# Row tiles of the second matmul in pairs and two rounds, convolution jobs ahead of the copies out

One kernel on one core of a Trainium2 chip. The metric is the device time in microseconds (us), the median over executions of the same program; the kernel before takes 698.73 us (6 executions, 698.49 to 698.90).

## The reference

A light convolution over time (7 taps, softmax weights per head), then a feed-forward block with a leaky ReLU:

```python
w = softmax(weight)                                 # [8 heads, 7 taps]
out[b, s, h, :] = sum_k w[h, k] * x[b, s + k - 6, h, :]   # x is [8, 4096, 192]
h = out.reshape(32768, 192) @ w_in                  # w_in  [192, 2048]
g = maximum(0.01 * h, h)
result = g @ w_out                                  # w_out [2048, 192]
```

## The kernel before

DVE (VectorE) does the convolution, PE (TensorE) both matmuls, ACT (ScalarE) the Prelu between them. The work is cut into 37 groups: ten half groups (256 time steps of two batches, `T = 256`), then 27 full ones (`T = 512`). In each step of the loop PE does two blocks of the first matmul (`mm1`), and then a quota of "slots" of the second matmul for the group before. Both matmuls use row tiling: the 128 rows of the array work as two tiles of 64 rows, which run beside each other.

A sum `po[n]` of the second matmul (128 tokens by 192 outputs) needs 16 chunks of 128 rows, each split into the upper and the lower 64. Both kernels keep the two row tiles out of each other's PSUM bank (the prediction names the page that asks for it). In the kernel before row tile 0 goes first through sum n, and row tile 1 follows 24 slots later; by then row tile 0 is in the bank of sum n+1 or n+2. A manual dependency, the "seal", makes row tile 1's first matmul wait for a Prelu that comes after row tile 0's last.

```python
    LAG = NFC + NFC // 2                 # NFC = 16: 24 slots
    ...
    LAST = NSUB - 2 * SUB - 1            # 247 of 256 sums go by row tiles
    ...
    def mm1(grp, u):
        ...                              # 12 matmuls, then the Prelu `act`
        while unsealed:
            seal[unsealed.pop()] = act.ins.name

    def mm2_slot(q):
        n, fc = divmod(q, NFC)
        if n < LAST:
            mm2_one(0, n, fc)            # row tile 0
        t1 = q - LAG
        if t1 >= 0:
            mm2_one(1, *divmod(t1, NFC)) # row tile 1; at fc == 0 it waits for seal[n]
            if t1 % NFC == NFC - 1:
                evac_o(t1 // NFC)        # copy out of PSUM: ACT in half groups, then DVE
    ...
        per = -(-len(ahead) // (steps - 1)) if T == ST else -(-len(ahead) // steps)
        for j in range(steps):
            ...                          # two blocks of mm1
            for _ in range(quota):
                mm2_slot(slot)
                slot += 1
            for job in ahead[per * j : per * (j + 1)]:
                job()                    # convolution of the next group, on DVE
    ...
    while slot < LAST * NFC + LAG:       # row tile 1 alone
        mm2_slot(slot)
        slot += 1
    for n in range(LAST, NSUB):          # the last sums with all 128 rows
        ...
```

## Time and profile before

| | before |
|---|---|
| time, median | 698.73 us |
| span of the profiled execution | 697.6 us |
| PE, DVE, ACT busy | 99%, 78%, 73% |

A line of the timeline or of the costliest groups has the source line, engine, operation and tiles; `x32` is a count. In the timeline the first number is the start and the second the time to the last end, both in us. PE's ends overlap the next starts, so I take a part's length from its start to the start of what follows. What to see before is shown in the prediction.

### The profile page before, as it was taken

What the parts mean: (1) busy time and instruction counts of PE and PEld (TensorE: products, weight loads), DVE (VectorE), ACT (ScalarE), POOL (GpSimd) and SP (SyncE); (2) the same over time, 40 slices, a digit from 0 to 9 for tenths busy, and PEclk for the clock granted to TensorE, in tenths of its full rate; (3) what the DMA queues carried; (4) which work ended last, traced back from release to release, by engine and by line L of the source; (5) the groups of instructions that cost most, each with busy time, mean ns of one, the idle gap of its engine ahead of it and who ended that gap; (6) DMA issues with size and microseconds to landing.
All of it is one profiled execution on the core that took longest, in us unless ns stands there. A gap on an engine that the chain in (4) does not pass through costs nothing.

```text
span 697.6 us, 26016 instructions
## 1 busy us (share of the span) xinstructions
PE 689.2 (99%) x11762; PEld 608.4 (87%) x11762; DVE 543.1 (78%) x1005; ACT 512.2 (73%) x576; POOL 139.6 (20%) x195
## 2 busy tenths in 40 slices
PE   8999999999999999999999999999999999999997
PEld 6799998678888888888888888888888888888887
DVE  6899999967777787777787777787777787777712
ACT  6788887977777777777777777777777777777770
POOL 3632221410222210222211222210222211000000
PEclk9999999999999999999999999999999999999999
DMA  9988553845566545556635556634566626122112
GB/s 171 108 97 96 83 77 77 85 72 81 73 71 92 81 69 81 70 72 90 84 65 82 68 77 85 87 69 75 76 75 82 91 63 77 55 52 58 47 36 70
DMA packets 184015, 54.39 MB, mean 78 GB/s; under 512 B 148320, under 2 KB 183136, under 8 KB 183904
## 3 DMA queue, kind: packets, MB, share of 16 engines
q0 software_dynamic: 97936, 14.17, 29.1%
q1 hardware_dynamic: 85968, 38.56, 22.6%
q8 instruction: 92, 1.51, 0.9%
q14 instruction: 19, 0.16, 0.1%
HBM read 29.88 MB, written 25.17 MB: 79 GB/s over the span
## 4 chain that ended last, share of the span: by engine, by line
PE 86%; DVE 11%; DMA 2%; ACT 1%; issue 1%; SPq 0%; ACTq 0%
PE po L388 43%; PE ph L367 41%; DVE yt L181 9%; DMA x_nat<-in_x_dram 1%; ACT g L374 1%; DVE yt L175 1%; PE acc L200 1%; PE warm L249 1%; DMA xt<-x_bf 1%; PE ptr L142 0%; DVE x_bf L127 0%; ACT x_bf L127 0%; DVE diag L296 0%; ACT yt L329 0%; SPq L430 0%
## 5 line engine op out<-in xcount | busy, mean ns | idle before, releaser
L374 ACT ACTIVATE g<-ph 128x1024 bf16<-128x1024 f32 x512 | 496.3, 1021 | 163.0 <-PE ph L367 163.0
L181 DVE SCALAR_TENSOR_TENSOR yt<-xt,wk,yt 128x512 bf16<-128x512 bf16 (+1 forms) x648 | 442.5, 683 | 17.6
L388 PE MATMUL po<-w_out,g 64*128 64x192 bf16 (+1 forms) x8048 | 397.9, 243 | 0.0
L388 PEld LDWEIGHTS <-g 64*128 64x128 bf16 (+1 forms) x8048 | 371.9, 94 | 29.0 <-issue 0.2
L367 PE MATMUL ph<-yt,w_in 64*128 64x512 bf16 (+1 forms) x3552 | 391.7, 347 | 2.1 <-ACT g L374 0.9
L367 PEld LDWEIGHTS <-w_in 64*128 64x128 bf16 x3552 | 247.4, 94 | 48.9 <-issue 5.6
L78 POOL DMA_DIRECT2D x_bf<-in_x_dram x180 | 133.6, 773 | 420.7 <-DMA xt<-x_bf 418.2
L427 DVE COPY o_sb<-po 128x192 f32<-128x192 f32 x216 | 77.3, 358 | 127.2 <-PE po L388 124.9
L175 DVE TENSOR_SCALAR yt<-xt,wk 128x512 bf16<-128x512 bf16 (+1 forms) x108 | 36.4, 337 | 0.3 <-DMA xt<-x_bf 0.3
L427 ACT COPY o_sb<-po 128x192 f32<-128x192 f32 x40 | 13.0, 325 | 0.0
L249 PE MATMUL warm<-zero 128*128 128x256 bf16 x24 | 5.8, 404 | 1.1 <-DVE junk L217 1.1
L200 PE MATMUL acc<-xt,diag 64*64 64x256 bf16 x84 | 6.6, 318 | 0.0
L200 PEld LDWEIGHTS <-diag 64*64 64x64 bf16 x84 | 5.2, 126 | 1.3 <-DVE xt L156 0.4
L249 PEld LDWEIGHTS <-zero 128*128 128x128 bf16 x24 | 2.8, 134 | 2.5 <-DVE junk L217 1.1
L304 ACT ACTIVATE diag<-ident,whm 128x64 bf16<-128x64 bf16 x14 | 3.6, 336 | 1.9 <-DVE whm L290 1.9
L156 DVE COPY xt<-ptr 128x384 bf16<-128x384 bf16 x7 | 2.2, 353 | 1.9 <-PE ptr L142 1.8
L474 POOL COPY pjunk<-g 1x1 bf16<-1x1 bf16 x1 | 0.2, 177 | 16.5 <-ACT g L374 16.5
L142 PEld LDWEIGHTS <-x_bf 64*128 64x128 bf16 x48 | 1.1, 101 | 2.7 <-ACT x_bf L127 1.9
L142 PE MATMUL ptr<-ident,x_bf 64*128 64x64 bf16 x48 | 1.6, 202 | 1.5 <-ACT x_bf L127 0.9
L127 DVE CAST x_bf<-x_nat 128x384 bf16<-128x384 f32 x5 | 2.3, 453 | 0.7 <-DMA x_nat<-in_x_dram 0.7
L329 ACT ACTIVATE yt<-acc,rsum 128x256 bf16<-128x256 f32 x2 | 0.9, 474 | 2.5 <-PE acc L200 2.5
L237 POOL DMA_DIRECT2D w_in<-in_moe_w_in_dram x4 | 2.6, 659 | 0.0
(34 smaller groups left out, 13.1 us busy)
## 6 DMA issues: line engine op xcount, KB each, us to landing
out_dram<-o_sb SPq DMA_DIRECT2D x128, 192.0 KB, 2.1
x_bf<-in_x_dram POOLq DMA_DIRECT2D x180, 64.0 KB, 3.1
x_nat<-in_x_dram SPq DMA_DIRECT2D x8, 192.0 KB, 4.3
w_in<-in_moe_w_in_dram POOLq DMA_DIRECT2D x4, 384.0 KB, 9.5
xt<-x_bf SPq DMA_TRANSPOSE x90, 2.4
w_out<-in_moe_w_out_dram POOLq DMA_DIRECT2D x1, 768.0 KB, 16.2
w<-in_weight_dram SPq DMA_DIRECT2D x1, 0.2 KB
```

Of the source, the lines that this page charges most:

```text
L78: nc.gpsimd.dma_start(out=t[:, c, :, e, :], in_=src[2 * rp + e, :, :, c * CH : (c + 1) * CH],)
L142: nc.tensor.transpose(out=ts[i][:, s, c, :], in_=x_bf[q // 2][ps, c, (q % 2) * HS + s, :, :].rearrange("p e k -> p (e k)"), identity=ident ...
L175: lambda s=src, d=dst, c=c: nc.vector.tensor_scalar_mul(d, s, wk[:, c, 0:1])
L181: lambda s=src, d=dst, c=c, k=k: nc.vector.scalar_tensor_tensor(out=d, in0=s, scalar=wk[:, c, k : k + 1], in1=d, op0=mybir.AluOpType.mult, ...
L200: lambda k=k, p=p, a=a, e=e, ps=ps: nc.tensor.matmul(out=acc[ps, :T], lhsT=diag[c][ps, p, k, :], rhs=xt[0][ps, c, a : a + T], start=(k == ...
L237: nc.gpsimd.dma_start(out=w_in[e * CH : (e + 1) * CH, :, fs], in_=moe_w_in[:, fs].rearrange("(c p) f -> p c f", p=CH),)
L249: nc.tensor.matmul(out=wa[:, 0, 0:HT], lhsT=zero[:, 0:128], rhs=zero, start=True, stop=True)
L304: nc.scalar.activation(out=diag[c][:, 1, k, :], in_=ident2, func=mybir.ActivationFunctionType.Copy, scale=whm[:, c, 1, k : k + 1],)
L367: nc.tensor.matmul(out=ph[:, e, i * T : (i + 1) * T], lhsT=w_in[ps, c, f * 128 : (f + 1) * 128], rhs=y[ps, c, t0 : t0 + T], start=(c == 0) ...
L374: act = nc.scalar.activation(out=g[blk][:, nf * u : nf * (u + 1), :, t0 : t0 + T], in_=ph.rearrange("p e (i t) -> p i e t", i=nf), func=my ...
L388: ins = nc.tensor.matmul(out=po[m], lhsT=g[b][ps, fc, e, s * 128 : (s + 1) * 128], rhs=w_out[ps, fc, :], start=(rt != 1 and fc == 0), stop ...
L427: copy(out=o_sb[:, n % 2, :], in_=po.pop(n))
```

## The change

Sums go in pairs through two rounds of 16 slots. In round 0 row tile 0 works on the first sum of the pair and row tile 1 on the second; in round 1 they change places. Both leave their banks at the same time, so there is no offset. Between the rounds stands one wait, for the copy out of the pair before. In full groups the convolution jobs stand ahead of the copies in DVE's order, spread over all eight steps.

```diff
-    LAG = NFC + NFC // 2
-    LAST = NSUB - 2 * SUB - 1
+    LAST = NSUB - 2 * SUB
...
+        p, fc = divmod(q, 2 * NFC)
+        rnd, fc = divmod(fc, NFC)
+        pair = (2 * p, 2 * p + 1)
+        first, last = fc == 0, fc == NFC - 1
...
+        for rt in range(2):
+            ins = mm2_one(
+                rt, pair[rt ^ rnd], fc, first and rnd == 0, last and rnd == 1
+            )
+            if first and rnd == 1:
+                sync(ins, seal, "both row tiles have left these banks")
+        if last and rnd == 0:
+            seal_round(p, ins)           # seal = evac_o(2 * p - 1), which waits for ins
+        if last and rnd == 1:
+            evac_o(pair[0])
...
+            if T == ST:
+                jobs = ahead[len(ahead) * j // steps : len(ahead) * (j + 1) // steps]
+                for job in jobs:
+                    job()
             for _ in range(quota):
                 mm2_slot(slot)
                 slot += 1
...
-    while slot < LAST * NFC + LAG:
-        mm2_slot(slot)
-        slot += 1
+    evac_o(LAST - 1)
```

More of the change, by code (lines that the diff above doesn't have):

```diff
@@ L345 @@
     evac_first(1, nc.vector.tensor_copy, nc.vector.tensor_copy)
-    g, po, osb, seal = {}, {}, {}, {}
+    g, po, osb, seal = {}, {}, {}, None
     subs = [
@@ L353 @@
     NSUB = len(subs)
-    LAST = NSUB - 2 * SUB - 1
-    unsealed = []
+    LAST = NSUB - 2 * SUB
     def mm1(grp, u):
@@ L378, in mm1, with sync, mm2_one @@
         )
-        while unsealed:
-            seal[unsealed.pop()] = act.ins.name
-        return act
-    def mm2_one(rt, m, fc):
+        return act
+    def sync(after, first, why):
+        tc.add_manual_dep(
+            after.ins, first.ins.name,
+            mybir.DependencyInfo(
+                mybir.DependencyClass.Sync, mybir.DependencyReason.DATA
+            ),
+            reason=why,
+        )
+    def mm2_one(rt, m, fc, start, stop):
         b, e, s = subs[m]
-        if rt != 1 and fc == 0:
-            po[m] = psum_o.tile([128, D], FP32, name="po", tag="po")
         ps = slice(0, 128) if rt is None else slice(rt * CH, (rt + 1) * CH)
-        ins = nc.tensor.matmul(
+        return nc.tensor.matmul(
             out=po[m],
@@ L391, in mm2_one, with mm2_slot, seal_round @@
             rhs=w_out[ps, fc, :],
-            start=(rt != 1 and fc == 0),
-            stop=(rt != 0 and fc == NFC - 1),
-        )
-        if rt == 0 and fc == NFC - 1:
-            unsealed.append(m)
-        if rt == 1 and fc == 0:
-            tc.add_manual_dep(
-                ins.ins, seal[m],
-                mybir.DependencyInfo(
-                    mybir.DependencyClass.Sync, mybir.DependencyReason.DATA
-                ),
-                reason="other row tile, same bank",
-            )
-    def mm2_slot(q):
-        n, fc = divmod(q, NFC)
-        if n < LAST:
-            mm2_one(0, n, fc)
-        t1 = q - LAG
-        if t1 >= 0:
-            mm2_one(1, *divmod(t1, NFC))
-            if t1 % NFC == NFC - 1:
-                evac_o(t1 // NFC)
+            start=start,
+            stop=stop,
+        )
+    def mm2_slot(q):
+        p, fc = divmod(q, 2 * NFC)
+        rnd, fc = divmod(fc, NFC)
+        pair = (2 * p, 2 * p + 1)
+        first, last = fc == 0, fc == NFC - 1
+        if first and rnd == 0:
+            for n in pair:
+                po[n] = psum_o.tile([128, D], FP32, name="po", tag="po")
+        for rt in range(2):
+            ins = mm2_one(
+                rt, pair[rt ^ rnd], fc, first and rnd == 0, last and rnd == 1
+            )
+            if first and rnd == 1:
[4 more added lines that the diff above has]
+            evac_o(pair[0])
+    def seal_round(p, ins):
+        nonlocal seal
+        if p == 0:
+            seal = nc.scalar.copy(out=junk, in_=junk)
+        else:
+            seal = evac_o(2 * p - 1)
+        sync(seal, ins, "between the rounds")
     def evac_o(n):
@@ L426, in evac_o @@
         copy = nc.scalar.copy if b < NHALF else nc.vector.tensor_copy
-        copy(out=o_sb[:, n % 2, :], in_=po.pop(n))
+        ins = copy(out=o_sb[:, n % 2, :], in_=po.pop(n))
         if n % 2 == 1:
@@ L433, in evac_o @@
             )
+        return ins
     pjunk = const_pool.tile([1, 1], BF16)
@@ L447 @@
             ahead = conv_jobs(groups[i + 1]) if i + 1 < len(groups) else []
-        per = -(-len(ahead) // (steps - 1)) if T == ST else -(-len(ahead) // steps)
+        per = -(-len(ahead) // steps)
         for j in range(steps):
@@ L462 @@
                     cast_first(3, u - 2, nc.scalar.copy)
+            jobs = ahead[per * j : per * (j + 1)]
+            if T == ST:
+                jobs = ahead[len(ahead) * j // steps : len(ahead) * (j + 1) // steps]
+                for job in jobs:
+                    job()
+                jobs = []
             for _ in range(quota):
@@ L477 @@
                 transpose_x(2)
-            for job in ahead[per * j : per * (j + 1)]:
+            for job in jobs:
                 job()
@@ L489 @@
         avail += 2 * T // 128 * NFC
-    while slot < LAST * NFC + LAG:
-        mm2_slot(slot)
-        slot += 1
+    evac_o(LAST - 1)
     for n in range(LAST, NSUB):
+        po[n] = psum_o.tile([128, D], FP32, name="po", tag="po")
         for fc in range(NFC):
-            mm2_one(None, n, fc)
+            mm2_one(None, n, fc, fc == 0, fc == NFC - 1)
         evac_o(n)
```

## The prediction

> **What bounds the kernel now.** I read the page first: busy shares, costliest groups, then the waits, then the timeline of single steps, and at the end the tail.
>
> ```profile
> PE 689.2 (99%) x11762; PEld 608.4 (87%) x11762; DVE 543.1 (78%) x1005; ACT 512.2 (73%) x576; POOL 139.6 (20%) x195
> L181 DVE SCALAR_TENSOR_TENSOR yt<-xt,wk,yt 128x512 bf16<-128x512 bf16 (+1 forms) x648 | 442.5, 683 | 17.6
> L388 PE MATMUL po<-w_out,g 64*128 64x192 bf16 (+1 forms) x8048 | 397.9, 243 | 0.0
> L367 PE MATMUL ph<-yt,w_in 64*128 64x512 bf16 (+1 forms) x3552 | 391.7, 347 | 2.1 <-ACT g L374 0.9
> L427 DVE COPY o_sb<-po 128x192 f32<-128x192 f32 x216 | 77.3, 358 | 127.2 <-PE po L388 124.9
> ```
>
> PE is busy 99% of the span and its two matmul lines wait 2.1 us in all; DVE's copies out wait for PE, not the other way. So PE sets the time, and the question is only whether it runs slots faster, or fewer of them. The timeline of PE in a stretch of full groups shows a step: 12 matmuls of 512 columns, then 16 slots of two 192-column matmuls, one per row tile.
>
> ```profile
> 402.02 1.56 PE L388 MATMUL po<-w_out,g 64*128 64x192 bf16 x32
> 403.34 1.53 PE L367 MATMUL ph<-yt,w_in 64*128 64x512 bf16 x12
> 404.64 1.56 PE L388 MATMUL po<-w_out,g 64*128 64x192 bf16 x32
> ```
>
> From start to start: the second matmul's 16 slots take 403.34 - 402.02 = 1.32 us, that is 82.5 ns a slot; the first's 12 take 1.30. A step is 2.62 us, with no gap between its parts. There are 256 steps, some 670 us of the 698.75. The chain that ended last shows the same, with one odd round:
>
> ```profile
> 660.33 1.29 PE ph L367 x12
> 661.63 1.36 PE po L388 x32
> 662.99 1.29 PE ph L367 x12
> 664.28 1.32 PE po L388 x32
> ```
>
> The first round of a full group takes 1.36 us instead of 1.32. The reason stands in the timeline of another such round: the Prelu ahead of it starts after 0.74 us of idleness, not 0.66 to 0.68, and it is the Prelu that "seals" a half-sum: row tile 1 may enter the bank in the middle of the round only when it is done.
>
> ```profile
> 409.56 1.94 ACT L374 ACTIVATE g<-ph 128x1024 bf16<-128x1024 f32 x2 [0.74 <-PE ph L367]
> 409.87 1.60 PE L388 MATMUL po<-w_out,g 64*128 64x192 bf16 x32
> ...
> 412.15 1.94 ACT L374 ACTIVATE g<-ph 128x1024 bf16<-128x1024 f32 x2 [0.66 <-PE ph L367]
> 412.52 1.56 PE L388 MATMUL po<-w_out,g 64*128 64x192 bf16 x32
> ```
>
> Such rounds come once a group, 20.96 us apart, from 200.27 to 661.39 us: (661.39 - 200.27) / 20.96 + 1 = 23 rounds.
>
> Last the tail. The row tiles run 24 slots apart, so row tile 1 has 24 slots left alone once row tile 0 is through; then 9 sums follow with all 128 rows, 144 matmuls:
>
> ```profile
> 679.81 14.13 PE L388 MATMUL po<-w_out,g 64*128 64x192 bf16 x168
> 681.88 11.83 PEld L388 LDWEIGHTS <-g 128*128 128x128 bf16 x144 [0.16 <-issue]
> 693.98 0.36 DVE L427 COPY o_sb<-po 128x192 f32<-128x192 f32 x1 [0.96 <-PE po L388]
> ```
>
> The lone slots start at 679.81 and the full ones at 681.88: 2.07 us for 24 slots of half work, 86 ns each, about the price of a whole pair.
>
> **What the Trainium skill says.** "TensorE: Matmul & The Clock Gate", section "Back-to-back issue gap", gives N / 2.4 + 2.5 ns: 82.5 ns for 192 columns, which is the slot of this trace to the digit, and 215.8 for 512 (1.295 us for six pairs; trace 1.30). Nothing is left to gain in a full slot. "TensorEngine Tiling (Array Packing)", section "Restrictions and Gotchas", says that different row tiles may not access one PSUM bank at the same time and software must see to it: hence the seal before, and the two rounds with a wait between them after. The trace agrees only in that the two tiles' slots do run beside each other with two banks open. The same page, "Key Properties", says a change of tiling mode drains the array; the trace has one change to 128 rows at the end, with 0.16 us of idle weight load. The change keeps exactly one. "Perfetto Trace Analysis", section "Identifying the Most-Contended Engine", warns that matmul busy time is a poor roofline measure; so I rest on start-to-start times, not on 99%.
>
> **The change, part by part.**
>
> 1. *No offset between the row tiles.* Pairs start and end together, so no lone slots. At the start this saves nothing: the loop gives a fixed 16 slots to each step of the second group, filled or half filled, and that stretch ends in a wait of 0.87 us for a cast on ACT. At the end: before, 24 lone slots plus 9 full sums of 16 = 168 slots after the last paired round; after, 16 paired slots (round 1 of the last pair, in the last step) plus 8 full sums = 144. Saved 24 x 82.5 ns = 1.98 us, and some 0.08 us more of the slower lone start. **-2.0 us**.
> 2. *The seal moves from the Prelu to the copy out.* The 0.04 us of 23 rounds goes, because a round's first slot no longer depends on the Prelu: **-0.9 us**. The new wait: round 1 needs a copy that itself waits for round 0's last matmul. But quotas are 16 slots a step (8 in one group), so rounds end with the step, and two first-matmul blocks, 1.30 us, lie before the next round. A copy now starts about 0.28 us after the start of the last matmul it waits for (its 243 ns and some 40), and takes 0.36: the seal is ready about 0.64 us after the round. Slack about 0.6 us. In the half groups ACT copies (0.33 us) and its next Prelu comes late enough: the same slack. **0**.
> 3. *Conv jobs ahead of the copies.* 21 jobs over 8 steps instead of 7, at most three multiply-adds a step. On DVE three of them follow each other in about 0.78 us and the copy occupies 0.27: 3 x 0.78 + 0.27 = 2.60 us of a step of 2.62. So DVE arrives at its copy just on time in the worst step, and does not fall behind. The last three jobs of a group end about 0.25 us after the last round; the first matmul of the new group that needs their chunk starts 0.43 us after it, and DVE to PE takes about 0.05 us where the trace shows such a wait. Slack about 0.12 us. **0**.
> 4. *Small things.* 16 matmuls more (one sum moves from full to half rows), already in part 1; one copy of 1 column on ACT in the second group, which idles 0.69 us there. Copies, transfers and bytes are unchanged. PE's instructions that wait fall from 1034 to 735 in the built program; satisfied waits show no cost in 1.32 us rounds that hold one. **0**.
>
> Sum: 698.75 - 2.0 - 0.9 = **695.8 us**, 0.4% faster, well within 2%.
>
> **The rivals.**
>
> *The seal becomes a wait.* If DVE comes to the copies over 0.6 us late, round 1 stalls. For it: three-job steps leave only 0.01 us. Against: they are never more than two in a row, then a short step follows, and before already fits three jobs and a copy in a step (idle before copies still sums to 124.9 us). A stall of 0.1 us in each of some 100 pairs of the full groups would be +10 us, about 706.
>
> *Groups start on late jobs.* Slack is only 0.12 us, and before the jobs had a whole step in hand. If the last job came 0.2 us after it is needed at 26 group starts, +5 us: about 701. Against: DVE's durations are the same to a few ns from group to group, and DMA-fed waits of these jobs sum to 0.3 us. An input arriving late would hit here first, since jobs start about 1.4 us earlier than now.
>
> *The tail gains nothing or more.* If the end hung on transfers out, the 2 us would vanish: 697.8. Against: 0.96 us idle before each copy of the tail, waiting for PE. If the lone slots at the start also cost, up to 2 us more: 694.
>
> **Range and chances.** The base is 695.8. Both new waits can only add, and their slack is known to about 0.1 us, so the range reaches further up: 695.0 to 697.6. Faster by over 2% would need 14 us and no view offers that: 0.01. Slower by over 2% needs a stall of over 0.1 us at every round: 0.02. Within 2%: 0.97.
>
> **What would show it.** Right: the chain has no 1.36 us rounds at group starts; the tail's matmuls are 128 full ones directly after a first-matmul block and one paired round; line L388's successor has 8064 matmuls; idle time of PE stays near 2 us. Wrong: first-matmul blocks longer than 1.30 us at group starts with DVE's conv line as releaser (part 3), or rounds longer than 1.32 us or starting late, with a DVE copy as releaser (part 2).

## More of the kernel before

To compare traces I cut PE's work at six starts that the timeline shows in every one: the first slot; the first `mm1` block of 512 columns; nine steps later, the second step of the second full group; the last `mm1` block; the last matmul; the end.

## The result

The kernel after takes 696.08 us (median of 6, 695.24 to 696.88), 2.65 us less. The ratio is 0.9961 with a 95% interval of 0.9948 to 0.9974. Ratios here are the mean time of one kernel's runs over that of the other's of the same rounds, so not quite the ratio of the medians. It is a gain clear of noise, well inside 2%, and 0.3 us from the predicted 695.8.

The busy line and three of the costliest groups after; the columns are busy us, mean ns of one, then idle time before them and what ended it.

```profile
PE 683.7 (99%) x11778; PEld 539.4 (78%) x11778; DVE 543.9 (78%) x1005; ACT 516.4 (74%) x577; POOL 139.7 (20%) x195
L391 PE MATMUL po<-w_out,g 64*128 64x192 bf16 (+1 forms) x8064 | 382.7, 243 | 0.0
L365 PE MATMUL ph<-yt,w_in 64*128 64x512 bf16 (+1 forms) x3552 | 379.3, 347 | 2.7 <-DMA w_in<-in_moe_w_in_dram 1.1
L438 DVE COPY o_sb<-po 128x192 f32<-128x192 f32 x216 | 77.1, 357 | 121.5 <-PE po L391 115.5
```

PE still fills 99%, with 16 matmuls more, and nothing on DVE or ACT has become the bound. The second matmul's line has no idle time: the new wait between rounds never shows. The chain that ended last, in the same part of the kernel as the one shown of before:

```profile
655.71 1.29 PE ph L365 x12
657.00 1.32 PE po L391 x32
658.32 1.29 PE ph L365 x12
659.62 1.32 PE po L391 x32
660.94 1.29 PE ph L365 x12
662.23 1.32 PE po L391 x32
```

No 1.36 us round is left. The timeline at a group start tells why: the Prelu is as late as before (0.74 us of idleness), but the round takes 1.32 us, from 408.40 to 409.72. It is the first round of its pair, and none of its matmuls and weight loads carries a wait in the trace. (In the trace of before, row tile 1's matmul of the ninth slot of such a round starts at 410.64, 0.06 us after the end of the Prelu that it waits for.) The wait stands at the head of the second round, whose first weight load starts at 410.80 and first matmul at 411.01; the copy that it waits for starts at 409.94 and is done at 410.29.

```profile
408.03 1.94 ACT L372 ACTIVATE g<-ph 128x1024 bf16<-128x1024 f32 x2 [0.74 <-PE ph L365]
...
408.40 1.50 PE L391 MATMUL po<-w_out,g 64*128 64x192 bf16 x32
...
409.94 0.36 DVE L438 COPY o_sb<-po 128x192 f32<-128x192 f32 x1 [1.21 <-PE po L391]
...
411.01 1.50 PE L391 MATMUL po<-w_out,g 64*128 64x192 bf16 x32
```

And the tail, in the timeline of PE and of the weight loads:

```profile
677.75 12.16 PE L391 MATMUL po<-w_out,g 64*128 64x192 bf16 x160
679.17 10.51 PEld L391 LDWEIGHTS <-g 128*128 128x128 bf16 x128 [0.16 <-issue]
```

One paired round (32 matmuls) and 128 full ones, where before 24 lone matmuls preceded 144. The six stretches of the two profiled executions:

| stretch, us | before | after | difference |
|---|---|---|---|
| start to first slot | 23.92 | 23.37 | -0.55 |
| to the first 512-column block | 94.59 | 94.60 | +0.01 |
| nine steps | 20.30 | 19.79 | -0.51 |
| full groups, to the last `mm1` block | 539.63 | 538.69 | -0.94 |
| to the last matmul | 15.25 | 13.21 | -2.04 |
| to the end | 3.87 | 3.88 | +0.01 |
| span | 697.56 | 693.54 | -4.02 |

The profiles differ by 4.0 us where the medians differ by 2.65, because the profiled execution before took 699.26 us (above its median) and the one after 695.24 (the fastest of six). The extra lies in the first and third rows. The question for the experiments is which of these rows the change made.

### The profile page after: what moved, and what is told of

Read it like the earlier page. It is cut to its first block, busy times and chain, and to the rows that moved or that the text cites. A ratio compares the mean times of both kernels' runs of the same rounds, so it can differ in the third digit from the quotient of the medians.

```text
span 693.5 us, 26049 instructions
## 1 busy us (share of the span) xinstructions
PE 683.7 (99%) x11778; PEld 539.4 (78%) x11778; DVE 543.9 (78%) x1005; ACT 516.4 (74%) x577; POOL 139.7 (20%) x195
## 4 chain that ended last, share of the span: by engine, by line
PE 93%; DMA 3%; DVE 2%; ACT 1%; POOL 0%; issue 0%; SPq 0%; POOLq 0%; DVEq 0%
PE po L391 48%; PE ph L365 45%; DVE yt L180 2%; DMA w_in<-in_moe_w_in_dram 1%; DMA x_nat<-in_x_dram 1%; DMA xt<-x_bf 1%; ACT g L372 0%; POOL sel L226 0%; DVE yt L174 0%; ACT x_bf L126 0%; POOL w_in L236 0%; PE ptr L141 0%; DVE x_bf L126 0%; SPq L441 0%; POOL sel L224 0%
## 5 line engine op out<-in xcount | busy, mean ns | idle before, releaser
L391 PEld LDWEIGHTS <-g 64*128 64x128 bf16 (+1 forms) x8064 | 352.2, 94 | 45.3 <-issue 0.2
L391 PE MATMUL po<-w_out,g 64*128 64x192 bf16 (+1 forms) x8064 | 382.7, 243 | 0.0
L365 PE MATMUL ph<-yt,w_in 64*128 64x512 bf16 (+1 forms) x3552 | 379.3, 347 | 2.7 <-DMA w_in<-in_moe_w_in_dram 1.1
L365 PEld LDWEIGHTS <-w_in 64*128 64x128 bf16 x3552 | 186.5, 94 | 98.1 <-issue 4.6
L199 PE MATMUL acc<-xt,diag 64*64 64x256 bf16 x84 | 5.2, 270 | 0.5 <-DVE xt L155 0.5
```

The costliest lines, as they stand in the source:

```text
L199: lambda k=k, p=p, a=a, e=e, ps=ps: nc.tensor.matmul(out=acc[ps, :T], lhsT=diag[c][ps, p, k, :], rhs=xt[0][ps, c, a : a + T], start=(k == ...
L365: nc.tensor.matmul(out=ph[:, e, i * T : (i + 1) * T], lhsT=w_in[ps, c, f * 128 : (f + 1) * 128], rhs=y[ps, c, t0 : t0 + T], start=(c == 0) ...
L391: return nc.tensor.matmul(out=po[m], lhsT=g[b][ps, fc, e, s * 128 : (s + 1) * 128], rhs=w_out[ps, fc, :], start=start, stop=stop,)
```

## The experiments

My theory: the change is worth two terms, 0.94 us for the seal and 2.04 us for the tail; the start-up and the nine steps vary by themselves; the new wait and the new order cost nothing, because they have slack. The rivals: the 1.36 us rounds had another cause; lone slots cost something else than a full slot; the wait between rounds costs nothing in any position; the order of the jobs is a part of the gain.

### The seal alone: 25 slots apart instead of 24

The kernel before, with one edit:

```diff
-    LAG = NFC + NFC // 2
+    LAG = NFC + NFC // 2 + 1
```

> The kernel before with the row tiles 25 slots apart instead of 24. Theory (two separate savings: the seal's 0.04 us in 23 rounds, and 82.5 ns for each lone slot): the slot that waits for the Prelu comes 82.5 ns later, which is more than the 40 ns that it is late, so the 1.36 us rounds become 1.32 (23 x 0.04 = 0.92 us less), and one lone slot is added at the end (0.08 us more): 698.73 - 0.84 = 697.9 us. Rival (the 1.36 us rounds have another cause at group starts, such as the weights of the first round or the reuse of the g buffer by PE itself): they stay at 1.36 and the time is 698.8.

Measured: 698.48 us (697.47 to 699.11), ratio to before 0.9993, interval 0.9981 to 1.0006. The times alone say nothing, as they scatter by 1.6 us. The trace does: the full groups take 538.69 us, 0.94 less than before and to the digit what the kernel after takes. None of its 208 full rounds from the first 512-column block on is longer than 1.32 us. From its chain, where the round at 661.45 is the first of a group:

```profile
658.83 1.32 PE po L388 x32
660.15 1.29 PE ph L367 x12
661.45 1.32 PE po L388 x32
662.76 1.30 PE ph L367 x12
664.06 1.32 PE po L388 x32
```

So the 0.04 us were the wait for the Prelu; one slot more of distance removes it as well as the new scheme does. The interval of the ratio (1.3 us less to 0.4 us more) holds both the 0.84 us expected and no change. In the profiled execution the gain is hidden by the first slot, which came at 25.02 us, 1.1 later than in the profile of before: from 14.89 us on the granted clock was 0.50 for 3.4 us, and there 24 matmuls of `mm1` took 2.74 us, where before took 1.75.

### The price of a lone slot: 40 slots apart

```diff
-    LAG = NFC + NFC // 2
+    LAG = 2 * NFC + NFC // 2
```

> The kernel before with the row tiles 40 slots apart instead of 24. Theory: the seal lies a whole step before the slot that needs it, so no 1.36 us round is left (0.92 us less), and the tail has 40 lone slots, 16 more at 82.5 ns (1.32 us more): 698.73 - 0.92 + 1.32 = 699.1 us, and against the run with 25 slots 15 x 82.5 ns = 1.24 us more. The tail's matmuls from the last first-matmul block on: 40 lone slots in about 3.4 us, of which 16 in the last step. Rival (lone slots cost half, as they do half the work): 15 x 41 ns = 0.6 us more than with 25, 698.5 us. Rival (the offset at the start costs as well): 2.5 us more than with 25, about 700.4.

Measured: 700.18 us (699.02 to 700.57), ratio 1.0015, interval 1.0002 to 1.0027. Weight loads of the tail with 25 slots apart, then with 40:

```profile
679.38 2.21 PEld L388 LDWEIGHTS <-g 64*128 64x128 bf16 x25
681.74 2.34 PEld L388 LDWEIGHTS <-g 128*128 128x128 bf16 x29 [0.16 <-issue]
```

```profile
678.16 3.44 PEld L388 LDWEIGHTS <-g 64*128 64x128 bf16 x40
681.76 2.26 PEld L388 LDWEIGHTS <-g 128*128 128x128 bf16 x28 [0.16 <-issue]
```

From the first lone load to the first full one: 2.36 and 3.60 us. The 15 more lone slots cost 1.24 us, 82.7 ns each: the price of a full slot for half the work, as expected. The full groups take 538.69 us here too. The stretch between the first slot and the first 512-column block takes 94.36 us, so lone slots at the start cost nothing. The medians of these two runs differ by 1.70 us instead of 1.24, within their scatter; the profiled executions (699.11 and 699.28 us) differ by only 0.17, because the late first slot of the one with 25 (25.02 us against 23.73) takes up the 1.24.

### The wait between rounds without cover

The kernel after, with all rounds moved by 8 slots, so that a round ends in the middle of a step and the next one follows at once:

```diff
-        quota = (avail - slot) // steps
+        quota = (avail - slot - (8 if i > 1 else 0)) // steps
...
-            for _ in range(quota):
+            for _ in range(quota - (8 if i == 1 and j == 0 else 0)):
...
+    while slot < LAST * NFC:
+        mm2_slot(slot)
+        slot += 1
     evac_o(LAST - 1)
```

> The kernel after with its rounds moved by 8 slots, so that they end in the middle of a step and the next round follows at once, with no first matmuls between. Theory (the wait between the rounds is free only because 1.30 us of first matmuls cover it): every round 1 stalls for the copy: 0.28 us to its start, 0.36 us, 0.05 us to PE, so about 0.69 us in some 104 pairs of the full groups (72 us), and about 1.1 us in some 20 pairs of the half groups, where the copy stands behind two Prelus on ACT (22 us): about 790 us, rounds of 16 slots split into two parts with a gap of 0.7 us. Rival (PE's hardware or the early weight load hides the wait, or the copy is quicker seen from PE): under 720 us.

Measured: 780.91 us (780.41 to 780.99), ratio to before 1.1173. PE's timeline in a step, then two lines of the waits (us in total, times, longest):

```profile
433.87 0.82 PE L391 MATMUL po<-w_out,g 64*128 64x192 bf16 x16
435.15 0.83 PE L391 MATMUL po<-w_out,g 64*128 64x192 bf16 x16 [0.46 <-DVE o_sb L438]
435.82 1.46 PE L365 MATMUL ph<-yt,w_in 64*128 64x512 bf16 x12
```

```profile
PEld L391 <- DVE o_sb L438: 70.4, 103, 0.7
PEld L391 <- ACT o_sb L438: 20.8, 18, 1.2
```

Eight slots would take 0.66 us; the second eight start 1.28 us after the first eight. The stall is 0.62 to 0.64 us a pair in the full groups (the stretch grows by 604.27 - 538.69 = 65.6 us) and in the half groups it comes 18 times, and longer, from ACT (there the stretch grows by 113.50 - 94.60 = 18.9 us). Together 84.5 of the 84.8 us between the medians. The wait is real, and only its place makes it free. The sum was 9 us too high, 6 of them in the full groups: with both row tiles in step a copy starts 0.21 to 0.22 us after the round, not 0.28, so the wait is 0.22 + 0.36 + 0.05 = 0.63 us.

### Slack at the group starts

The kernel after, with one more multiply on DVE ahead of the last step's jobs:

```diff
                 jobs = ahead[len(ahead) * j // steps : len(ahead) * (j + 1) // steps]
+                if j == steps - 1 and jobs:
+                    nc.vector.tensor_scalar_mul(extra, extra, wk[:, 0, 0:1])
                 for job in jobs:
```

> The kernel after with one idle 128x512 multiply more on DVE ahead of the last step's conv jobs, in each of the 26 full groups that has a successor (0.38 us from start to start on DVE). Theory (group starts have only about 0.12 us of slack for the last conv job, as DVE's three-job steps fill 2.60 of 2.62 us): the first block of first matmuls of each group grows by 0.38 - 0.12 = 0.26 us: 26 x 0.26 = 6.8 us, about 702.9 us. Rival (DVE has more room than the sums of one step say, as it is busy for 78% only): no change, 696.1 us.

Measured: 697.85 us (696.52 to 698.41), ratio to before 0.9983, interval 0.9970 to 0.9995. The full groups take 540.59 us, 1.90 more than after, where the theory has 25 x 0.26 = 6.5 (25 of the 26 group starts lie in this stretch). The timeline around a group start:

```profile
407.19 0.35 DVE L484 TENSOR_SCALAR extra<-extra,wk 128x512 bf16<-128x512 bf16 x1
...
407.45 2.32 DVE L180 SCALAR_TENSOR_TENSOR yt<-xt,wk,yt 128x512 bf16<-128x512 bf16 x3
...
409.31 1.55 PE L365 MATMUL ph<-yt,w_in 64*128 64x512 bf16 x12
```

The block takes 1.55 us to its last end instead of 1.47: 0.08 of stall, and 1.90 / 25 = 0.08 on average. The multiply delays the jobs by 407.45 - 407.19 = 0.26 us, not 0.38, because the job after it does not depend on it. So the slack was 0.26 - 0.08 = 0.18 us, not 0.12; the missing 0.06 is again the copy that starts earlier. The trace of the kernel after agrees: around the same group start its last job ends at 407.30, 0.05 us of signal follow, and the matmul that waits for it starts at 407.54, which leaves 0.19. The theory's mechanism holds and both its sizes were off.

### The order of the jobs

The kernel after, again on one chip with the three runs that follow, and the same with the jobs behind the copies as before:

```diff
-        per = -(-len(ahead) // steps)
+        per = -(-len(ahead) // (steps - 1)) if T == ST else -(-len(ahead) // steps)
...
-            if T == ST:
-                jobs = ahead[len(ahead) * j // steps : len(ahead) * (j + 1) // steps]
-                for job in jobs:
-                    job()
-                jobs = []
```

> The kernel after, unchanged, on the chip of the runs beside it. Theory: what differs between its executions lies before the second full group (start-up and the wait of the first full groups for DVE); the stretch from the second full group's second step to the last first-matmul block is 538.7 us again and the tail the same, while the time may lie anywhere from 695.2 to 697. Rival (the steady part varies): the 538.7 us stretch differs by over 0.3 us.

> The kernel after with the conv jobs of full groups behind the copies again, three a step in the first seven steps, as in the kernel before. Theory (a job group behind the copy of step j runs in the same time as one ahead of the copy of step j+1, as both follow that copy; the order buys nothing): the same time as the kernel after within 0.3 us in the stretch of full groups, no stall at group starts. Rival (the order is needed to keep the copies or the last jobs in time): first-matmul blocks over 1.30 us at the group starts or late rounds, at least 0.1 us in each of 26 groups, 2.6 us more.

Measured: 696.10 us for the kernel after (694.89 to 696.52) and 696.00 for the old order (695.19 to 696.24); ratios to before 0.9957 and 0.9958. Full groups: 538.69 us in both; tail: 13.22 in both. The order buys nothing. The kernel after repeats its steady part to the digit, while its first slot came at 24.02 us and the nine steps took 20.43, where the first profile of it had 23.37 and 19.79. So the rows "start" and "nine steps" of the table vary from one execution of the same kernel to the next, by as much as they differed between the kernels. One thing inside the nine steps I can't assign: at the start of the second full group the block of `mm1` takes 1.81 us in this profile of the kernel after, with 0.34 us of waiting for DVE's convolution, and 1.29 with the old order; but the first 512-column block is shorter in turn (1.97 against 2.14 us). Two executions don't settle whether the order makes that.

### How late the seal may come

The kernel after with multiplies on DVE behind the copy that ends the first round of each full group but the first and the last; the last multiply is the seal. The first attempt, with two and with three multiplies:

```diff
             seal = evac_o(2 * p - 1)
+            if late:                     # first step of a full group
+                for _ in range(2):       # or 3
+                    seal = nc.vector.tensor_scalar_mul(extra[0], extra[0], wk[:, 0, 0:1])
         sync(seal, ins, "between the rounds")
```

> The kernel after with two idle 128x512 multiplies in a chain on DVE behind the first copy between rounds of each of 25 full groups, the second of which becomes the seal. Theory (slack of about 0.65 us, counted to the first matmul of the next round): seal at 0.22 + 0.275 + 0.383 + 0.347 = 1.23 us after the round, 0.05 more to PE, 1.28 against 1.295: no stall or under 0.03 us a group, under 0.8 us in all, about the time of the kernel after. Rival (the weights of the next round's first matmul are loaded some 0.2 us early and it is this load that waits): up to 0.2 us in each of 25 groups, 5 us more.

> As the run with two, with three multiplies in the chain. Theory: seal at 1.61 us after the round, 1.66 at PE against 1.295: 0.37 us of stall in each of 25 groups, 9.2 us more than the kernel after, about 705.5 us, and the stall stands ahead of the second round's first weight load with a DVE line as releaser. Rival (slack larger than 0.65 us): less than 4 us more.

Measured: 695.89 and 696.58 us, full groups 538.69 and 539.07 us. These two miss their aim: the wait for the round's end went with the name `seal` to the last multiply alone, so the copy and the other multiplies ran ahead of it. In the first of the two traces the copy starts at 409.75, inside the round that starts at 409.50, and only the last multiply waits, to 411.04. Nothing about slack follows. The mended version makes the copy wait too:

```diff
             if late:
+                sync(seal, ins, "between the rounds")
                 for _ in range(2):       # or 3
```

> Mends the run with two multiplies, where the copy and the first multiply were free to run before the round's end: now the copy waits for it too, and the two stand in a chain behind the copy. Theory (slack counted to the first matmul of the next round): seal at 0.22 + 0.275 + 0.383 + 0.347 = 1.23 us after the round, 1.28 at PE against 1.295: no stall, 538.7 us in the steady stretch. Rival (the early weight load waits and its lead is lost): up to 0.2 us in each of 25 groups, 543.7 us in that stretch.

> As the run with two in a true chain, with three. Theory: seal at 1.61 us after the round, 1.66 at PE against 1.295: 0.37 us of stall in each of 25 groups, 9.2 us more in the steady stretch than 538.7, about 547.9 us, and some 705.3 us in all. Rival (slack over 1 us): no change.

Measured: 702.88 us (ratio 1.0057, 1.0043 to 1.0070) and 713.75 us (1.0212, 1.0195 to 1.0229); full groups 546.03 and 555.91 us. A group of the run with three in which the multiplies keep their usual length, then one in which they don't:

```profile
441.09 1.46 PE L366 MATMUL ph<-yt,w_in 64*128 64x512 bf16 x12
...
441.57 1.12 DVE L433 TENSOR_SCALAR extra<-extra,wk 128x512 bf16<-128x512 bf16 x3
...
442.75 0.77 PEld L392 LDWEIGHTS <-g 64*128 64x128 bf16 x20 [0.69 <-DVE extra L433]
```

```profile
395.91 3.70 POOL L77 DMA_DIRECT2D x_bf<-in_x_dram  x5 [0.35 <-issue]
...
397.26 1.46 PE L366 MATMUL ph<-yt,w_in 64*128 64x512 bf16 x12
...
397.75 1.99 DVE L433 TENSOR_SCALAR extra<-extra,wk 128x512 bf16<-128x512 bf16 x3
```

In the first, the next round starts 442.75 - 441.09 = 1.66 us after the round, to the digit what was expected. With two multiplies an undisturbed group (PE's block at 541.95, next round at 543.27) takes 1.32 against 1.295: 0.03 us, where none was expected, as the two multiplies took 0.78 us and not 0.73. The rival's 0.2 us for the weight load did not come. So slack is counted to the first matmul, and a seal may come some 0.66 us later than the copy's (0.63 against 1.295 us) before anything is lost. The weight load waits, and its early start is then lost, but the matmul follows it at once: both are at 442.75 in that trace.

The totals were too low because of what the second fence shows: the multiplies can take longer. Counted from the end of each group's last multiply plus 0.05 us, the stalls add up to 7.0 us with two multiplies and 16.8 with three; the stretch grew by 7.3 and 17.2. In the second fence, where POOL issues DMAs at the time, the three multiplies take 1.99 us instead of 1.12. Over the run with two, the same multiply takes 343 ns at least, 454 in the median and 715 at most. In the trace records of these two runs and of the kernel after, no such multiply of 512 columns without a POOL issue beside it is longer than 354 ns. The reverse does not hold: 22 of the convolution's own multiplies in the kernel after have a POOL issue beside them, and their median is 345 ns. The convolution's multiply-adds (753 ns at most in the kernel after) and the copies stay as they are. The Trainium skill, "SBUF — State Buffer", section "Who interferes with whom", says that copies, casts and `tensor_scalar` on VectorE can, in their two-port modes, take a port pair that GpSimd shares, as an exclusive lock. The lengths agree with it for `tensor_scalar`; no run here takes POOL's issues away, so the cause is argued and not shown.

### An attempt at a faster version: six blocks of half groups

```diff
-    NHALF = 5
+    NHALF = 6
```

> The kernel after with six blocks of half groups instead of five, as an attempt at a faster version. Theory (the wait of the first full groups for DVE's convolution, 19.8 to 20.7 us for nine steps that PE alone would do in 18.3, comes from DVE's lag in the half groups; two more half groups let it gain some 0.2 us a step on PE): 0.3 to 0.8 us less than the kernel after, 695.5 us, with less spread. Rival (that stretch is held by ACT's two Prelus and the copies, not by DVE): the same time within 0.3 us, or 0.1 us more for the shorter matmuls.

Measured: 695.10 us (693.74 to 695.34), ratio to before 0.9941, interval 0.9929 to 0.9953. In PE's waits the kernel after, on the chip of the order test, has

```profile
PE ph L365 <- DVE yt L180: 0.8, 2, 0.5
```

and this version has no such line. That alone says little, as the first profile of the kernel after has none either. The length of the first 512-column block says more: 1.29 us here, without a stall, and 1.47 to 2.73 us in every other profile, except for the run with rounds in mid-step (1.29), whose half groups take 18.9 us longer. That fits the theory: slower or more half groups let DVE gain on PE. The nine steps from that block on take 19.24 us, against 19.79 and 20.43 in the two profiles of the kernel after; from the first slot to the last `mm1` block it is 652.65 us, against 653.08 and 653.72, so 0.4 to 1.1 us less. The intervals of the two ratios touch (0.9929 to 0.9953, and 0.9944 to 0.9970 for the kernel after in its own rounds), and the two were not run beside each other, so a gain over the kernel after is likely and not settled. It beats the kernel before, clear of noise.

## Why the prediction was right

The range held and so did the sum: -2.93 us predicted, -2.65 measured between medians, -2.98 in the two rows of the trace that the change made.

- **Part 1, the tail, -2.0 us.** Measured -2.04 (15.25 to 13.21). The price per lone slot holds when their number is changed: 1.24 us for 15. The prediction's 86 ns per lone slot is a little high: the lone matmuls start 82.5 ns apart in the trace of before, and 0.09 of the 2.07 us lie at the change to 128 rows, which the kernel after has too. The 0.06 us by which the tail gained more than 24 slots lies in the last `mm1` block, 1.37 us before and 1.30 after; why is open. That lone slots at the start cost nothing holds too: 94.59 and 94.60 us, and 94.36 with 40 slots apart.
- **Part 2, the seal, -0.9 us.** Measured -0.94, and the same by moving the old seal by one slot, so the cause named is the cause. The words "a round's first slot" are loose: the slot that waited is the ninth, in the middle of the round, as the prediction itself says where it reads the timeline. "Slack about 0.6 us": 0.66 by the mended chain of two and three multiplies, since the copy starts 0.06 us earlier than I took from the offset scheme.
- **Part 3, the jobs, 0.** Right as a sum (though 3 x 0.78 + 0.27 is 2.61, not 2.60). "Slack about 0.12 us" measured 0.18. What I did not see: this part of the change is not needed. A job group behind one copy and the next group ahead of the next copy follow the same instruction, so both orders are nearly the same program for DVE.
- **Part 4, 0.** No sign of a cost: 16 matmuls more are within part 1, and PE's rounds are 1.32 us. That nothing was left to gain in a full slot came true as well, but the prediction took the formula for the limit of a stream, which its section does not call it (see the list at the end); the trace bears it out.
- **The rivals.** In the full groups' steady part none came: no stall at rounds or group starts, and the end still follows the last matmul by 3.9 us. At one group start, the second full group's, the sign named for "wrong" did come: that block of `mm1` takes 1.60 us in the first profile of the kernel after and 1.81 in the second. There DVE had waited 1.9 and 2.0 us for an input by DMA some steps earlier, which fits the case that the prediction names ("an input arriving late would hit here first"). It costs 0.3 to 0.5 us once, inside the nine steps; before lost 0.1 there. The run with rounds in mid-step shows what the first rival costs with no cover at all: 85 us.
- **The base.** "Can only add" was not quite right about the range: the kernel after scatters by 1.6 us by itself, as the executions of before do in later rounds (697.59 to 700.03), which its first six (698.49 to 698.90) had hidden. That scatter sits ahead of the steady part: in the profiles the first slot came anywhere from 23.37 to 25.02 us, and the nine steps took 19.79 to 20.68 us (the run with rounds in mid-step and the one with six blocks left out). For the first slot the traces point to the granted clock. Its record opens, at full clock, at 10.7 us in the trace of before and at 4.5 in that of after; the first 28 convolution matmuls, which start at about 7.5 us, take 3.19 us before and 1.73 after, after which PE waits 1.1 us for the first weights. And the two latest first slots (25.02 us with 25 slots apart, 24.89 in the first attempt with three multiplies) are the two with 3.4 us at a clock of 0.50 from about 14.8 us on. Of the six executions of the kernel after, the three with a mean clock of 1.000 are the fastest (695.24 to 695.92) and the one with 0.997 the slowest (696.88). In the nine steps it is the first block of `mm1` (1.47 to 2.73 us) and the ninth (1.29 to 1.88) that vary; the waits listed there are for DVE's convolution. What decides either from one execution to the next stays open.

## What to carry to other kernels

When an engine is full, count its instructions at the seams: here every full slot already took its 82.5 ns before and after, and the whole gain was 24 half-empty slots at one end plus one wait of 40 ns, repeated 23 times. A dependency that needs another engine's answer is free where enough unrelated work of the waiting engine lies between, so put the seam of an accumulation where that work already stands; half a step further, the same wait cost 85 us. And when a change is worth less than the scatter of the start-up, compare steady stretches of traces, not times.

## What the Trainium skill lacked or had wrong

- "TensorE: Matmul & The Clock Gate", section "Back-to-back issue gap": this section calls N / 2.4 + 2.5 ns the isolated gap and gives other figures for sustained streams with weight loads (about 81 ns at N = 128 and 131 at N = 512). Here the formula is the sustained pace, with a weight load for each matmul and two row tiles: 1.32 us for 16 slots of 192 columns (82.5 ns) and 1.295 us for six pairs of 512 (216 ns).
- "TensorEngine Tiling (Array Packing)", "Key Properties": no price for the change of tiling mode. Here, at the one change from 64 to 128 rows, the weight loads pause 0.16 us, and the matmuls on either side start 0.175 us apart instead of 0.0825.
- The same page, "Restrictions and Gotchas": it asks for synchronization between row tiles but gives no figure for one. Here, round to copy to round: 0.22 + 0.36 + 0.05 = 0.63 us, wholly hidden behind 1.295 us of other matmuls.
- "SBUF — State Buffer", section "Who interferes with whom": no figure for a `tensor_scalar` beside POOL's DMA issues. Measured: 346 ns in the median without one, and up to 715 with one, though many beside one keep their length.
